# Two neighbouring tokens per partition, regrouping copies within SBUF and a written engine order in a chunked linear-attention and token-mixing kernel

## The chip, the cores and the metric

The kernel runs on one core of one Trainium2 chip. The metric is device time in microseconds of one execution. The kernel before took 166.44 us (median of 3 runs, 164.67 to 166.62).

## The reference

Inputs are `r`, `k`, `v`, `w` of shape (4 batches, 8 heads, 768 tokens, 48) in float32, a bonus `u` of (8, 48), and three small weight matrices. A recurrent linear attention with a decay per channel gives x of (4, 768, 384), and a token-mixing stage gives the output:

```python
for t in range(S):
    cur = np.einsum('bhd,bhe->bhde', u[None] * kt, vt)
    y[:, :, t] = np.einsum('bhd,bhde->bhe', rt, state + cur)
    state = wt[:, :, :, None] * state + np.einsum('bhd,bhe->bhde', kt, vt)
...
W_tok = scale * np.einsum('bsd,btd->bst', x @ w_q, x @ w_k)
mixed = np.einsum('bst,btd->bsd', W_tok, x)
out = np.maximum(mixed, 0.0) @ w_out
```

## The kernel before

The work is cut into 12 blocks of 256 tokens, three to a batch; a block holds two chunks of 128 tokens. For each block `load` (L119) issues eight transfers on the SP queue, two for each of w, k, r and v: 128 tokens on 128 partitions, eight heads of 48 float32 (rows of 192 bytes) each. The pool `ld` has four buffers, so loads can run four blocks ahead.

`prep` (L136) takes the logarithm of w on ACT (`logw`, L142). PE multiplies it with triangular matrices, which gives running sums over the tokens: `cw1` (exclusive) and `cw0` (inclusive, with eight column sums behind it). ACT takes their exponentials (`ecwx` L148, `emcw` L156, and the chunk's decay `pt` L158). DVE forms `Rd` = r times `ecwx` (L162), POOL forms `Kd` = k times `emcw` (L164), ACT casts v to bf16 (`VB`, L167).

`back` (L171) transposes `Rd` and `Kd` on PE (`psT`), DVE copies them out (`RKT`, L179), PE multiplies them to one score matrix `A` per chunk, and DVE masks it into `AmB` (L189, one instruction per chunk). POOL forms k·u (L194) and then ·r (L197) in `uk`, DVE reduces that to `diag` (L199), and POOL makes the bonus rows `Vd` (L201).

`scan` (L205) keeps the state `SB`: for each chunk PE makes `Sn` and the output `Y`, DVE evacuates them (L226, L238) into `X`. Then X is transposed (`xt_ps`, `XT` on ACT, L247) and projected (`qk`, `wk_s`, `wqT`). After a batch's third block `moe` (L260) runs: `Tps`, six `mps` with a Relu on ACT (`mixT`, L272), six `fps` evacuated by DVE and ACT in turn (`osb`, L280 and L282), and the stores on the ACT queue (L283).

PSUM is shared by tags of two buffers each: "big" holds `cw1`, `cw0`, `psT` and both `A`; "s" holds `Sn` and `Y`; "m" holds everything of the projections and of `moe`. A tile takes the buffer of the one before the last, and its first writer waits until that one's readers are done. The main loop (L288) calls `prep(n)` before `back(n - 1)`, so the order of "big" is the sums of block n, then `psT` and `A` of block n - 1. The order on each engine is otherwise chosen by the scheduler of the framework. The framework also gives each transfer of the SP and ACT queues one of eight completion semaphores in turn; a transfer waits until the transfer that had the semaphore before has landed, even when that one stands on the other queue.

Of the kernel before, what the change touches and what calls it, by code (L numbers as in the profile page):

```python
# [25 lines left out]
def kernel(  # L26
# [14 lines left out]
    C = 128  # L41
    NCH = S // C
    NP = H // 2
    NU = S // (2 * C)
# [9 lines left out]
    def mm(o, l, rr, start=True, stop=True, sgc=True, trans=False):  # L54
        nc.tensor.matmul(o, l, rr, start=start, stop=stop,  # L55
                         skip_group_check=sgc, is_transpose=trans)

    nc.scalar.preload_act_table_set("natural_log_exp_and_others")

    consts = ctx.enter_context(tc.tile_pool(name="consts", bufs=1))  # L60
    U128 = consts.tile([C, C], BF16, tag="U128")
    make_upper_triangular(nc, U128, 1.0, diag=True)
    US128 = consts.tile([C, C], BF16, tag="US128")
    make_upper_triangular(nc, US128, 1.0, diag=False)
    ID128 = consts.tile([C, C], BF16, tag="ID128")
    make_identity(nc, ID128)
    ones = U128[:, C - 1:C]

    iota0 = consts.tile([C, 1], mybir.dt.int32, tag="iota0")
    nc.gpsimd.iota(iota0, pattern=[[0, 1]], base=0, channel_multiplier=1)  # L70
    iota1 = consts.tile([C, 1], mybir.dt.int32, tag="iota1")
    nc.gpsimd.iota(iota1, pattern=[[0, 1]], base=1, channel_multiplier=1)
    bias_px = consts.tile([C, 1], F32, tag="bpx")
    bias_mi = consts.tile([C, 1], F32, tag="bmi")
    bias_c = consts.tile([C, 1], F32, tag="bc")
    nc.scalar.activation(bias_px, iota0, ACT.Copy, bias=0.0, scale=MU)
    nc.scalar.activation(bias_mi, iota1, ACT.Copy, bias=0.0, scale=-MU)
    nc.gpsimd.memset(bias_c, MU * C)

    NB = 4
    LW, RdS, KdS, PT = [], [], [], []
    for i in range(NB):
        for lst, nm, e in ((LW, "logw", nc.gpsimd), (RdS, "RdS", nc.vector),
                           (KdS, "KdS", nc.gpsimd)):
            t = consts.tile([C, 2, NP, C], BF16, name=f"{nm}{i}", tag=f"{nm}{i}")
            e.memset(t, 0.0)
            lst.append(t)
        t = consts.tile([C, 2, H], F32, name=f"pt{i}", tag=f"pt{i}")  # L90
        nc.vector.memset(t, 0.0)
        PT.append(t)
# [8 lines left out]
    ld = ctx.enter_context(tc.tile_pool(name="ld", bufs=4))  # L101
# [6 lines left out]
    mout = ctx.enter_context(tc.tile_pool(name="mout", bufs=4))  # L108
# [4 lines left out]
    def stile(shape, dtype, name):  # L113
        return ps.tile(shape, dtype, name=name, tag="s", bufs=2)

    def big(shape, dtype, name):
        return ps.tile(shape, dtype, name=name, tag="big", bufs=2)

    def load(n):  # L119
        b, m = divmod(n, NU)  # L120
        G = {}
        for nm, ap in (("w", w), ("k", k), ("r", r), ("v", v)):
            t = ld.tile([C, 2, H, D], F32, name=nm + "G", tag=nm + "G")
            for c in range(2):
                nc.sync.dma_start(out=t[:, c], in_=ap[  # L125
                    b, :, ds((m * 2 + c) * C, C)].rearrange("h p d -> p h d"))
            G[nm] = t
        return G

    def chd(t):  # L130
        return t

# [3 lines left out]
    def prep(n, G):  # L136
        P = {}
        logw = LW[n % NB]
        Rd = RdS[n % NB]
        Kd = KdS[n % NB]  # L140
        pt = PT[n % NB]
        nc.scalar.activation(pad(logw), chd(G["w"]), ACT.Ln, bias=0.0, scale=LN_SCALE)  # L142
# [62 lines left out]
    def scan(n, P, st):  # L205
# [8 lines left out]
        for cc in range(2):  # L214
# [25 lines left out]
            if c + 1 < NCH:  # L240
                st["S"] = SB2
# [93 lines left out]
```

## Time and profile before

| | |
|---|---|
| median of 3 runs | 166.44 us |
| the profiled execution's own time | 165.66 us |
| its span in the profile | 163.9 us (1.76 us lie around it) |
| busy: PE, DVE, POOL, ACT | 104.8, 99.2, 95.7, 80.9 us |
| transfers of the SP queue | 100242 packets, 18.98 MB |
| stores | 24 of 192 KB, 2.0 us from issue to landing (median) |

In a row of the timeline the first number is the start in us, the second the length (of all the instructions, where the row ends in x2 or more), and a bracket tells how long the engine was idle before and what the profile holds for the releaser. In a row that groups instructions the columns are busy time in us, mean length in ns, idle time before and its releasers.

### The profile page before, as it was taken

Reading aid. Unit: us, or ns where it says so; the run is one execution under the profiler, and the core shown is the slowest. Engines: PE = TensorE matmul, PEld = TensorE weight load, DVE = VectorE, ACT = ScalarE, POOL = GpSimd, SP = SyncE. Lnnn points to the kernel's source line nnn. Section 1 sums busy time; section 2 is a strip of 40 time slices with the busy share of each in tenths; the row PEclk is TensorE's granted clock in tenths of the full one; section 3 lists DMA queues with packets and bytes.
Section 4 is the critical chain, followed back from the end, with each engine's and each line's share of the span. In section 5 each row is a group of like instructions: output and inputs, shape, how many; then the busy total and the mean of one; then the engine's idle time right before and its main releaser. Section 6 shows DMA issues by size and latency. Waiting matters only on the chain.

```text
span 163.9 us, 3082 instructions
## 1 busy us (share of the span) xinstructions
PE 104.8 (64%) x1196; PEld 70.8 (43%) x1196; DVE 99.2 (61%) x124; ACT 80.9 (49%) x152; POOL 95.7 (58%) x72
## 2 busy tenths in 40 slices
PE   0305103752379488994958898886589949857690
PEld 0203003441257365674637366665344527734240
DVE  4020203645668997899889978899582696670030
ACT  3535420430155576775729757793766342303721
POOL 7931009999994999598696952949960940000000
PEclk9999999999999999998799999699975995765967
DMA  5999999999999990289989969999970331000034
GB/s 111 194 187 187 190 187 186 182 210 172 192 183 190 167 175 0 72 221 268 194 165 190 174 173 256 220 197 187 159 140 0 110 125 59 4 0 0 0 127 161
DMA packets 104512, 24.23 MB, mean 148 GB/s; under 512 B 101041, under 2 KB 104498, under 8 KB 104498
## 3 DMA queue, kind: packets, MB, share of 16 engines
q1 hardware_dynamic: 100242, 18.98, 75.0%
q10 hardware_dynamic: 3456, 4.72, 8.2%
q0 software_dynamic: 800, 0.34, 1.7%
q8 instruction: 9, 0.15, 0.4%
q14 instruction: 5, 0.04, 0.1%
HBM read 19.66 MB, written 4.72 MB: 149 GB/s over the span
## 4 chain that ended last, share of the span: by engine, by line
PE 29%; SPq 16%; POOL 15%; DVE 14%; issue 10%; ACT 7%; DMA 6%; ACTq 0%; POOLq 0%
SPq L125 15%; DMA rG<-in_r_dram 6%; DVE AmB L189 6%; PE fps L55 6%; POOL uk L197 5%; PE Y L55 5%; POOL uk L194 4%; PE qk L55 3%; PE psT L55 3%; DVE RKT L179 3%; PE cw L55 3%; POOL KdS L164 3%; POOL Vd L201 3%; PE Tps L55 3%; ACT XT L247 2%
## 5 line engine op out<-in xcount | busy, mean ns | idle before, releaser
L164 POOL TENSOR_TENSOR KdS<-kG,emcw 128x768 bf16<-128x768 f32 x12 | 21.1, 1758 | 18.9 <-ACT emcw L156 11.1
L189 DVE TENSOR_TENSOR AmB<-A,US 128x1024 bf16<-128x1024 f32 x24 | 28.3, 1219 | 4.4 <-PE A L55 4.3
L162 DVE TENSOR_TENSOR RdS<-rG,ecwx 128x768 bf16<-128x768 f32 x12 | 17.2, 1433 | 14.5 <-DMA rG<-in_r_dram 13.4
L197 POOL TENSOR_TENSOR uk<-uk,rG 128x768 f32<-128x768 f32 x12 | 24.3, 2028 | 0.5
L201 POOL TENSOR_TENSOR Vd<-VB,diag 128x768 bf16<-128x768 bf16 x12 | 18.4, 1532 | 10.0 <-DVE diag L199 6.0
L194 POOL TENSOR_TENSOR uk<-kG,ubc 128x768 f32<-128x768 f32 x12 | 21.7, 1810 | 1.7 <-DMA kG<-in_k_dram 1.7
L179 DVE COPY RKT<-psT 128x2048 bf16<-128x2048 bf16 x12 | 14.6, 1218 | 11.1 <-PE psT L55 11.1
L247 ACT COPY XT<-xt_ps 128x768 bf16<-128x768 bf16 x12 | 9.6, 798 | 20.8 <-PE xt_ps L55 20.6
L238 DVE TENSOR_TENSOR X<-Y,Vd 128x384 bf16<-128x384 f32 x24 | 13.2, 552 | 9.2 <-PE Y L55 5.9
L55 PEld LDWEIGHTS <-KdS 128*128 128x128 bf16 x176 | 13.7, 113 | 11.5 <-POOL KdS L164 9.4
L55 PE MATMUL Y<-VB,AmB 128*128 128x48 bf16 x192 | 10.7, 199 | 11.7 <-DVE AmB L189 9.8
L148 ACT ACTIVATE ecwx<-cw,bias_px 128x768 bf16<-128x768 f32 x12 | 10.8, 902 | 14.2 <-PE cw L55 14.2
L55 PEld LDWEIGHTS <-RKT 48*128 48x128 bf16 (+1 forms) x272 | 12.3, 105 | 10.7 <-DVE RKT L179 7.4
L55 PE MATMUL fps<-wout_sb,mixT 128*128 128x384 bf16 x72 | 15.9, 365 | 0.7 <-ACT osb L282 0.3
L55 PE MATMUL cw<-logw,US 128*128 128x384 bf16 x24 | 8.2, 438 | 12.5 <-ACT logw L142 12.5
L55 PEld LDWEIGHTS <-AmB 128*128 128x128 bf16 x192 | 8.4, 107 | 17.6 <-DVE AmB L189 14.8
L55 PE MATMUL psT<-ID,KdS 128*128 128x128 bf16 x96 | 9.4, 242 | 9.1 <-POOL KdS L164 9.1
L199 DVE TENSOR_REDUCE diag<-uk 128x16 f32<-128x768 f32 x12 | 11.4, 946 | 6.3 <-POOL uk L197 6.3
L280 DVE COPY osb<-fps 128x384 f32<-128x384 f32 x12 | 6.7, 554 | 14.0 <-PE fps L55 14.0
L167 ACT CAST VB<-vG 128x768 bf16<-128x768 f32 x12 | 10.0, 830 | 10.3 <-DMA vG<-in_v_dram 10.1
L55 PE MATMUL A<-RKT 48*128 48x128 bf16 x192 | 10.5, 235 | 6.2 <-DVE RKT L179 5.6
L142 ACT ACTIVATE logw<-wG 128x768 bf16<-128x768 f32 x12 | 10.1, 843 | 6.6 <-DMA wG<-in_w_dram 6.5
(54 smaller groups left out, 196.9 us busy)
## 6 DMA issues: line engine op xcount, KB each, us to landing
wG<-in_w_dram SPq DMA_DIRECT2D x24, 192.0 KB, 4.6
kG<-in_k_dram SPq DMA_DIRECT2D x24, 192.0 KB, 4.5
rG<-in_r_dram SPq DMA_DIRECT2D x24, 192.0 KB, 4.5
vG<-in_v_dram SPq DMA_DIRECT2D x24, 192.0 KB, 4.7
out_dram<-osb ACTq DMA_DIRECT2D x24, 192.0 KB, 2.0
wout_sb<-in_moe_w_out_dram POOLq DMA_DIRECT2D x1, 288.0 KB, 6.1
wq_f<-in_moe_w_q_dram SPq DMA_DIRECT2D x1, 96.0 KB, 4.1
wk_sb<-in_moe_w_k_dram POOLq DMA_DIRECT2D x1, 48.0 KB, 4.3
```

The lines of the kernel that those rows point to most:

```text
L55: nc.tensor.matmul(o, l, rr, start=start, stop=stop, skip_group_check=sgc, is_transpose=trans)
L125: nc.sync.dma_start(out=t[:, c], in_=ap[b, :, ds((m * 2 + c) * C, C)].rearrange("h p d -> p h d"))
L162: nc.vector.tensor_tensor(pad(Rd), chd(G["r"]), ecwx.rearrange("p c (h d) -> p c h d", d=D), ALU.mult)
L164: nc.gpsimd.tensor_tensor(pad(Kd), chd(G["k"]), emcw.rearrange("p c (h d) -> p c h d", d=D), ALU.mult)
L179: nc.vector.tensor_copy(RKT, psT)
L189: nc.vector.tensor_tensor(AmB[:, c].rearrange("p q h t -> p h q t"), A, _rep(_rep(US128, 1, NP), 1, 2), ALU.mult)
L194: nc.gpsimd.tensor_tensor(uk, G["k"], _rep(ubc.rearrange("p (h d) -> p h d", d=D), 1, 2), ALU.mult)
L197: nc.gpsimd.tensor_tensor(uk, uk, G["r"], ALU.mult)
L199: nc.vector.tensor_reduce(diag, uk, axis=AX.X, op=ALU.add)
L201: nc.gpsimd.tensor_tensor(Vd, VB, _rep(diag, 3, D), ALU.mult)
L238: nc.vector.tensor_tensor(X[:, c], Y8, P["Vd"][:, cc].rearrange("p h d -> p (h d)"), ALU.add)
L247: nc.scalar.copy(XT[:, :, ds(m * 2 * C, 2 * C)], tp)
```

## The change

- **Layout.** A block's 256 tokens lie with tokens 2p and 2p+1 on partition p. One transfer per input and block then has rows of 384 bytes: `load` issues four per block instead of eight. Halves of the partitions now hold the two chunks. `ld` has three buffers instead of four.
- **Sums.** Over this layout PE needs two matmuls for each of three sums (`cwa`, two halves, and `cwb`), six per block instead of four; the exponentials are four instructions of 384 columns instead of two of 768.
- **Transposes** need nothing more: `trR` writes each transposed 128 columns to the two chunks' places.
- **Regrouping.** The second operand role of k, v and the bonus rows needs one chunk on 128 partitions. `Kd`, `VB` and `Vd` of a block stand side by side in one tile (`KdS`, 1280 columns), and `swap` copies it into `Kn` with four transfers of 64 partitions by 2560 bytes on the SP queue.
- **Stores** are two per pair of chunks, each from 64 partitions.
- **Set-up.** Only the gaps of the padded tiles are zeroed (256 columns of `KdS` on POOL, where `KdS` and `logw` had 1024 each); masks and biases follow the new layout. The load of `w_q` moves from the SP queue to POOL's.
- **Order.** Every step has a time in a table, and the instructions are written in the order of these times; the scheduler no longer moves them. A block is 8.3 units long; the sums of block n + 1 (at 9.2) come after the score matrices of block n (7.2 and 7.8).

```diff
-    ld = ctx.enter_context(tc.tile_pool(name="ld", bufs=4))
+    ld = ctx.enter_context(tc.tile_pool(name="ld", bufs=3))
...
+    def load(n, nm, ap):
+        b, m = divmod(n, NU)
+        src = ap[b, :, ds(m * C2, C2)]
+        t = ld.tile([C, H, D2], F32, name=nm + "G", tag=nm + "G")
+        nc.sync.dma_start(out=t, in_=src.rearrange("h (p j) d -> p h (j d)", j=2))
+        T[nm, n] = t
...
+    def sums(n):
+        lw = LW[n % NB]
+        lw4 = pad(lw)
+        cwa = big([C, 2, 512], F32, "cwa")
+        cwb = big([C, 2, 512], F32, "cwb")
+        for o, m0, m1 in ((cwa[:, 0], BS, BS), (cwa[:, 1], BI, BS), (cwb[:, 0], BI, BI)):
+            od = o[:, 0:DM].rearrange("p (h d) -> p h d", d=D)
+            mm(od, m0, lw4[:, 0], stop=False)
+            mm(od, m1, lw4[:, 1], start=False)
...
+    def exps(n):
+        cwa, cwb = T["cwa", n], T["cwb", n]
+        ex = hw.tile([C, 2, DM], BF16, name="ex", tag="ex")
+        em = hw.tile([C, 2, DM], BF16, name="em", tag="em")
+        nc.scalar.activation(em[:, 0], cwa[:, 1, 0:DM], ACT.Exp, bias=bias[2], scale=-1.0)
+        nc.scalar.activation(em[:, 1], cwb[:, 0, 0:DM], ACT.Exp, bias=bias[3], scale=-1.0)
+        nc.scalar.activation(ex[:, 0], cwa[:, 0, 0:DM], ACT.Exp, bias=bias[0], scale=1.0)
+        nc.scalar.activation(ex[:, 1], cwa[:, 1, 0:DM], ACT.Exp, bias=bias[1], scale=1.0)
...
+    def swap(n):
+        Kn = bt.tile([C, 2, KV], BF16, name="Kn", tag="Kn")
+        for q in range(2):
+            for j in range(2):
+                nc.sync.dma_start(out=Kn[ds(j * HC, HC), q],
+                                  in_=KdS[n % NB][ds(q * HC, HC), j])
...
+    def vd(n):
+        nc.gpsimd.tensor_tensor(vpart(KdS[n % NB], 1), vpart(KdS[n % NB], 0),
+                                _rep(T["diag", n], 3, D), ALU.mult)
...
+        steps = [
+            (-3.2, uk1, ()), (-0.7, log, ()), (0.2, uk2, ()), (0.9, sums, ()),
+            (2.0, exps, ()), (2.6, red, ()), (3.0, kdec, ()),
+            (3.9, decay, ()), (4.0, rdec, ()), (2.4, vcast, ()), (4.9, trR, (1,)),
+            (5.2, vd, ()), (5.4, trR, (0,)), (6.0, evT, ()), (6.8, swap, ()),
+            (7.2, amat, (0,)), (7.7, mask, (0,)), (7.8, amat, (1,)), (8.9, mask, (1,)),
+        ]
```

In this table `uk1` and `uk2` are the two products for the bonus, `kdec` and `rdec` make `Kd` and `Rd`, `trR` the transposes (1 for k, 0 for r), `evT` the copy to `RKT`, `amat` and `mask` the score matrix and its mask, `decay` makes `pt`. A second table puts `state` and `ymat` with their evacuations `stev` and `yev` 12.5 and more after a block's start, and the stage behind a batch (`tmat`, `mix`, `fin` with their evacuations) after its last block.

The rows below are instruction orders; a name's number tells buffers apart. **DVE, from one `AmB` of an early block to the next block's.** Before, `RdS_102` belongs to block 2 and stands ahead of the copy `RKT` of block 1:

```order
L189 TENSOR_TENSOR AmB<-A,US_64 128x2x4x128 x2
L199 TENSOR_REDUCE diag<-uk 128x16
L226 TENSOR_TENSOR SB_300<-Sn,pt_90 128x384
L162 TENSOR_TENSOR RdS_102<-rG,ecwx 128x16x48
L238 TENSOR_TENSOR X<-Y_284,Vd 128x384
L238 TENSOR_TENSOR X<-Y_302,Vd 128x384
L179 COPY RKT<-psT 128x2048
```

The same place now; `RdS_79` belongs to block 2, and so do the `RKT` and the `AmB` behind it:

```order
L226 TENSOR_TENSOR AmB<-A,MASK 128x2x4x128
L243 TENSOR_REDUCE diag<-uk 128x8x2
L175 TENSOR_TENSOR RdS_79<-rG,ex 128x16x48
L268 TENSOR_TENSOR SB_515<-Sn,pt_77 128x384
L296 TENSOR_TENSOR X<-Y,Kn 128x384
L211 COPY RKT<-psT 128x2048
L296 TENSOR_TENSOR X<-Y,Kn 128x384
L226 TENSOR_TENSOR AmB<-A,MASK 128x2x4x128
L268 TENSOR_TENSOR SB_574<-Sn,pt_77 128x384
```

What moved: the decayed r (and on PE the sums) of a block stood one block ahead of its transposes and now stand in the same block.

**ACT, in block 1**, where the weight `wq_sb` waits for its load, and `pt_77` is what frees the PSUM buffer of block 1's first score matrix:

```order
L188 CAST KdS_76<-vG 128x2x384
L415 ACTIVATE wq_sb<-wq_f 128x192
L169 ACTIVATE pt_77<-cwb,bias_c 48x4x2 x2
L137 ACTIVATE logw_78<-wG 128x16x48
L310 COPY XT<-xt_ps 128x3x256
```

Before, `pt_98` of block 1 stood ahead of `wq_sb`:

```order
L158 ACTIVATE pt_98<-cw_203,bias_c 48x8 x2
L167 CAST VB<-vG 128x768
L297 ACTIVATE wq_sb<-wq_f 128x192
L142 ACTIVATE logw_100<-wG 128x16x48
L167 CAST VB<-vG 128x768
```

What moved: `wq_sb` now stands between the cast of v and the two `pt` of block 1.

**ACT, in the block after the Relus of a batch** (`em` and `ex` are the exponentials of the next block):

```order
L310 COPY XT<-xt_ps 128x3x256
L367 COPY osb<-fps 128x384
L373 DMA out_dram<-osb 64x2x384 x2
L159 ACTIVATE em<-cwa,bias_67 128x384
L160 ACTIVATE em<-cwb,bias_68 128x384
L161 ACTIVATE ex<-cwa,bias_65 128x384
L162 ACTIVATE ex<-cwa,bias_66 128x384
L328 CAST wk_s<-qk 128x128
L329 CAST wqT<-qk 64x256
L188 CAST KdS_76<-vG 128x2x384
L367 COPY osb<-fps 128x384
```

What moved: one evacuation and two stores stand ahead of the exponentials, and the next evacuation behind the cast of v.

451 lines of the change are left out of this document (263 added, 188 removed).

## The prediction

> **What bounds the kernel now.** I read the queues first, then the masks as a clock of the blocks, then the idle time at the start. The page, and the SP queue's own waits and timeline:
>
> ```profile
> DMA  5999999999999990289989969999970331000034
> q1 hardware_dynamic: 100242, 18.98, 75.0%
> SPq L125 <- DMA out_dram<-osb: 15.5, 2, 11.3
> 57.14 1.55 SPq L125 DMA_DIRECT2D rG<-in_r_dram  x2
> 70.03 1.12 SPq L125 DMA_DIRECT2D vG<-in_v_dram  x2
> ```
>
> The transfer engines look like the bound: nines for 30 of 40 slices. But in slices 15 and 16 they are empty, because a load waited 11.3 us for a store's semaphore (from 58.7 to 70.0). What that full queue costs is read from the blocks. The DVE timeline, first and last masks, one quick pair, and the last X:
>
> ```profile
> 29.16 2.36 DVE L189 TENSOR_TENSOR AmB<-A,US 128x1024 bf16<-128x1024 f32 x2 [0.31 <-PE A L55]
> 47.10 2.36 DVE L189 TENSOR_TENSOR AmB<-A,US 128x1024 bf16<-128x1024 f32 x2 [1.35 <-PE A L55]
> 83.76 2.36 DVE L189 TENSOR_TENSOR AmB<-A,US 128x1024 bf16<-128x1024 f32 x2 [0.79 <-PE A L55]
> 91.61 2.36 DVE L189 TENSOR_TENSOR AmB<-A,US 128x1024 bf16<-128x1024 f32 x2
> 143.16 2.35 DVE L189 TENSOR_TENSOR AmB<-A,US 128x1024 bf16<-128x1024 f32 x2 [0.22 <-PE A L55]
> 146.43 0.56 DVE L238 TENSOR_TENSOR X<-Y,Vd 128x384 bf16<-128x384 f32 x1 [0.45 <-PE Y L55]
> ```
>
> Masks of the first block end at 31.5, of the last at 145.5: 114.0 us for 11 intervals, 10.4 each. One interval took 17.9, a quick one 7.85, so the middle is held near 8 by DVE and stretched by stalls. Ahead lie 31.5 us, behind 18.4. Why 31.5? The POOL timeline:
>
> ```profile
> 8.74 0.95 POOL L88 MEMSET KdS<- 128x1024 bf16 x1
> 15.90 0.68 POOL L293 PARTITION_BROADCAST ubc<-u  x1 [6.21 <-ACT ecwx L148]
> 24.40 3.23 POOL L164 TENSOR_TENSOR KdS<-kG,emcw 128x768 bf16<-128x768 f32 x2 [7.82 <-DMA kG<-in_k_dram]
> ```
>
> POOL idles 6.2 us before the broadcast and 7.8 us behind it. The inputs of the first `KdS` were there long before 24.4: k of block 0 was issued by 3.4. [...]
>
> **The change part by part. Start.** [...] POOL's set-up shrinks: of eight fills of 0.95, four remain with a quarter of the columns, and some nine small mask instructions come, so it ends near 5.5 instead of 9.7 (estimate). Then 6.2 + 0.7 + 7.8 gives 20.2. The bonus products now stand ahead of `Kd`; their prices and those of the block's chain:
>
> ```profile
> L194 POOL TENSOR_TENSOR uk<-kG,ubc 128x768 f32<-128x768 f32 x12 | 21.7, 1810 | 1.7 <-DMA kG<-in_k_dram 1.7
> L201 POOL TENSOR_TENSOR Vd<-VB,diag 128x768 bf16<-128x768 bf16 x12 | 18.4, 1532 | 10.0 <-DVE diag L199 6.0 <-ACT wqT L257 2.0 <-ACT VB L167 1.9
> 80.48 1.65 POOL L164 TENSOR_TENSOR KdS<-kG,emcw 128x768 bf16<-128x768 f32 x1 [1.63 <-ACT emcw L156]
> L189 DVE TENSOR_TENSOR AmB<-A,US 128x1024 bf16<-128x1024 f32 x24 | 28.3, 1219 | 4.4 <-PE A L55 4.3
> L179 DVE COPY RKT<-psT 128x2048 bf16<-128x2048 bf16 x12 | 14.6, 1218 | 11.1 <-PE psT L55 11.1
> L226 DVE TENSOR_TENSOR SB<-Sn,pt 128x384 bf16<-128x384 f32 x20 | 11.0, 549 | 0.2
> L199 DVE TENSOR_REDUCE diag<-uk 128x16 f32<-128x768 f32 x12 | 11.4, 946 | 6.3 <-POOL uk L197 6.3
> L272 ACT ACTIVATE mixT<-mps 128x384 bf16<-128x384 f32 x24 | 10.8, 489 | 2.1 <-PE mps L55 1.7
> 85.43 0.49 PE L55 MATMUL cw<-logw,US 128*128 128x384 bf16 x2
> 71.80 0.61 PE L55 MATMUL psT<-ID,KdS 128*128 128x128 bf16 x8
> 74.71 0.42 PE A L55 x8
> ```
>
> Two products 3.6, `Kd` 1.65, transposes 0.7 with the hops, `RKT` 1.2, `A` 0.5, two masks 2.35: the first masks end at **30.2**.
>
> **A plain interval.** This is the heart. Before, a block's sums and both decayed operands were made one block ahead. Now the order of the PSUM tag is sums, transposes, scores of the same block, and the second sum `cwb` of block n + 1 takes the buffer of the second `A` of block n. So one chain runs through every block, counted from the end of a second mask: two matmuls for `cwb` 0.6 with hops; one exponential of 384 columns 0.5 (like a Relu of that size): 1.1; `Kd` 1.7: 2.8. DVE's decayed r is ready at 2.0, but meets `Kd`:
>
> ```profile
> 70.89 1.82 POOL L194 TENSOR_TENSOR uk<-kG,ubc 128x768 f32<-128x768 f32 x1
> 71.00 2.52 DVE L162 TENSOR_TENSOR RdS<-rG,ecwx 128x768 bf16<-128x768 f32 x1
> 72.79 2.40 POOL L197 TENSOR_TENSOR uk<-uk,rG 128x768 f32<-128x768 f32 x1
> ```
>
> DVE's product began behind POOL's, ended 0.8 after it, and POOL's next was 0.6 longer: they exclude each other. So it ends at 3.65. `SB` and X of the block before follow in DVE's order (0.9): 4.55, hiding the transposes of r; `RKT` 1.2: 5.75; `A` 0.5: 6.25; mask 1.2; `SB` 0.4; mask 1.2: **9.05**; 8.6 where a block has no second `SB`. DVE's own work would fit in about 7.5, the sum of the same rows without the waits. There are two of the one, three of the other: 43.9. The bound above is POOL's next product slipping in first each time, 1.8 more; below, no exclusion, 0.8 less. I keep the middle row's order.
>
> **Intervals with a batch's stage.** Six of the eleven carry it. Prices:
>
> ```profile
> L167 ACT CAST VB<-vG 128x768 bf16<-128x768 f32 x12 | 10.0, 830 | 10.3 <-DMA vG<-in_v_dram 10.1
> L266 ACT CAST Tsb<-Tps 64x384 bf16<-64x384 f32 x4 | 1.9, 473 | 4.0 <-PE Tps L55 4.0
> L282 ACT COPY osb<-fps 128x384 f32<-128x384 f32 x12 | 5.8, 479 | 10.1 <-PE fps L55 8.1 <-DVE osb L280 2.0
> 68.02 0.86 ACTq L283 DMA_DIRECT2D out_dram<-osb  x2
> 82.60 0.80 PE qk L55 x9
> 70.00 0.50 PE fps L55 x3
> ```
>
> In the first (three of them) PE reaches the first `mps` only when ACT has cast v (to 3.2) and `Tsb` (3.7); `Sn`, `Y`, the transposes and two more `mps` follow in PE's order, so `RKT` starts at 5.8 instead of 4.55; three `mps`, `Sn` and `Y` then stand ahead of `A`: first mask at 7.75 instead of 6.25; one `osb` on DVE between the masks, 0.5: **11.05**. In the second, one `osb` and two store issues (0.5 + 0.9) stand ahead of the exponentials on ACT (+0.6); PE must pass four `fps` before `Sn`, the last waiting for the `osb` behind the cast of v (4.3), so the transposes end at 6.65; DVE waits for an `osb` before the decayed r, which then meets the next POOL product (to 5.2) and ends at 6.05; `RKT` at 6.95: **11.5**. Together 3 x 22.55 = 67.65. Bounds: each at 9.05 if the slack swallows all, each 2 longer if the waits add.
>
> **Weights.** `wq_sb` stands ahead of `pt` of block 1 on ACT and waits for a load that POOL issues only behind `Kd` of block 1 (at 2.8).
>
> ```profile
> wk_sb<-in_moe_w_k_dram POOLq DMA_DIRECT2D x1, 48.0 KB, 4.3
> L158 ACT ACTIVATE pt<-cw,bias_c 48x8 f32<-48x8 f32 x24 | 6.2, 260 | 1.3 <-DVE osb L280 1.1
> ```
>
> Landing at 7.1, `wq_sb` 0.4, two `pt` 0.5, `A` 0.5: first mask at 8.5 instead of 6.25, **+2.3** once (0 if the load lands within 2 us).
>
> **Loads and copies.** 384-byte rows move between 187 GB/s (nothing gained per byte: 8.4 us per block) and twice that (the packet as unit: 4.2). The nearest row is of stores in 1536-byte rows, the window from 155 to 164:
>
> ```profile
> GB/s 0 0 0 0 0 0 0 0 0 0 0 0 55 362 369 348 403 212 0 116 348 362 48 48 355 382 89 246 348 396 348 369 41 0 0 0 0 0 0 0
> out_dram<-osb ACTq DMA_DIRECT2D x24, 192.0 KB, 2.0
> wG<-in_w_dram SPq DMA_DIRECT2D x24, 192.0 KB, 4.6
> ```
>
> I take 4.2 to 6: hidden under 9 to 11 us of block. The four copies (0.66 MB, 1.8 us at the stores' rate) wait for `Vd`, which ends 2.4 us before an interval begins; PE wants the first two at 2.3, so 4.7 us later. A store lands in 2.0, a load in a full ring in 4.6: I take 2.6 for two copies, hidden; without that cover it costs one for one. On SP they stand ahead of the loads three blocks on, which have 12 us of slack; a load or copy can still wait for a store's semaphore, and this slack covers it. [...]
>
> **Tail.** 18.4 as before; the last two X now follow the last mask at once (+0.1), and the last store leaves as a pair behind the last evacuation: 0.4 for another issue and some 0.6 of transfer. **19.5**.
>
> **Sum.** 30.2 + 43.9 + 67.65 + 2.3 + 19.5 = 163.55 of span; the profiled execution lay 1.76 over its span (165.66), so 165.3; said as **165**. That execution lies 0.8 under the median of 166.44, and 2% of that, about what a measurement of this kernel can tell, is 3.3 us.
>
> **Rivals.** (a) The written order hides the batch's stage: every interval stays near 9, and the weights land in time. 165.3 - 6 intervals' excess of 13.35 - 2.3 = 150. For it: DVE has 1.5 us free per block and ACT and PE more. Against: PE, ACT and DVE each take their instructions in order, and the named waits stand ahead of the transposes. (b) POOL's gaps are waits for inputs after all: `Kd` of block 0 would start near 10.6 (k landed by 7, two products 3.6) instead of 23.8: 152. Against: the inputs were there. (c) Slower: the copies land late. [...] It decides from 4.7 us after `Vd`. For it: copies and loads share the ring. Against: the ring is mostly empty by then. (d) 384-byte rows gain nothing per byte: 8.4 + 3.5 for the copies + 1 for stores = 12.9 per block, 180. Against: the stores' 348 to 403 GB/s.
>
> **How the numbers follow.** The forecast has 0.45: 0.30 within 2%, 0.10 faster and 0.05 slower, since its terms are uncertain by some 6 us (159 to 171, its own range). (a) 0.27, (b) 0.06, (c) 0.16, (d) 0.06. Faster: 0.10 + 0.27 + 0.06 = 0.43; within 2%: 0.30; slower: 0.05 + 0.16 + 0.06 = 0.27. The range goes from (a) to (c): 149 to 174, which leaves (d) and edges out.
>
> **What would show it.** Right: POOL's two gaps again, first masks ending near 30; `KdS` waiting for the exponential of `cwb` in every block; plain masks 9 apart and those with a batch's stage 11 to 12; the transfer digits no longer all nines; `Sn` not waiting for copies. Wrong: masks evenly 8 to 9 apart (a); first masks before 20 (b); PE waiting for `Kn` in plain blocks (c); loads landing later than 8 us behind their issue (d).

## The result and the profile after

The changed kernel took 175.03 us (median of 4 runs, 174.32 to 178.33) beside 165.56 for the kernel before on the same chip: ratio 1.056 (95% interval 1.044 to 1.069), so slower by some 9.5 us. The forecast was 165.0 with a range to 174. Later comparisons are ratios to the kernel before on the chip of that run, with runs of a disturbed clock left out; medians contain all runs.

The profiled execution took 175.48 us with a span of 173.7. First the lines that answer to those of before: the transfer engines and SP's queue on the page, and two DMA issue groups (KB each, median us from issue to landing).

```profile
DMA  5999300499794989947999898399965053740055
q1 hardware_dynamic: 53762, 26.75, 58.3%
...
Kn<-KdS SPq DMA_DIRECT2D x48, 160.0 KB, 2.8
...
out_dram<-osb ACTq DMA_DIRECT2D x24, 192.0 KB, 3.0
```

The transfers are no longer a wall of nines, although the queue now moves 26.75 MB with the copies instead of 18.98. POOL's timeline at the start:

```profile
4.11 1.07 POOL L406 MEMSET KdS<- 128x256 bf16 x4
12.21 0.68 POOL L411 PARTITION_BROADCAST ubc<-u  x1 [7.03 <-issue]
22.17 1.79 POOL L232 TENSOR_TENSOR uk<-kG,ubc 128x768 f32<-128x768 f32 x1 [9.29 <-issue]
...
25.80 1.64 POOL L185 TENSOR_TENSOR KdS<-kG,em 128x768 bf16<-128x768 f32 x1
```

Both gaps are there again, now with "issue" for a releaser, that is with nothing that the profile could name. They are larger: 7.03 and 9.29, together 16.3 where I had used 14.0. DVE's timeline, of the first block and then of a plain one:

```profile
25.88 0.95 DVE L243 TENSOR_REDUCE diag<-uk 128x16 f32<-128x768 f32 x1 [22.90 <-POOL uk L238]
26.75 1.50 DVE L175 TENSOR_TENSOR RdS<-rG,ex 128x768 bf16<-128x768 f32 x1
29.42 1.23 DVE L211 COPY RKT<-psT 128x2048 bf16<-128x2048 bf16 x1 [1.17 <-PE psT L58]
31.35 2.36 DVE L226 TENSOR_TENSOR AmB<-A,MASK 128x1024 bf16<-128x1024 f32 x2 [0.71 <-PE A L58]
...
54.41 1.22 DVE L226 TENSOR_TENSOR AmB<-A,MASK 128x1024 bf16<-128x1024 f32 x1
...
57.94 1.55 DVE L175 TENSOR_TENSOR RdS<-rG,ex 128x768 bf16<-128x768 f32 x1 [1.45 <-ACT ex L162]
...
62.06 2.36 DVE L226 TENSOR_TENSOR AmB<-A,MASK 128x1024 bf16<-128x1024 f32 x2
```

The first masks end at 31.35 + 2.36 = 33.71 (forecast 30.2). A block's second mask ends at 55.63 and the next one's at 64.42: 8.79 for a plain interval (forecast 8.6). The ends of all second masks, read in this way, cut the span into the windows of the next table. Its columns are the window, its length, the busy time and number of instructions of PE, PEld (PE's weight loads), DVE, ACT and POOL, TensorE's granted clock (PEclk, 1.00 is full speed), the share of the DMA engines and GB/s.

```profile
0.00:33.71 33.71, 6.27 (x50) 4.18 (x51) 7.91 (x28) 6.22 (x10) 15.64 (x32) 1.00 0.56 148
33.71:46.06 12.35, 8.33 (x83) 6.00 (x82) 7.95 (x10) 5.31 (x11) 9.18 (x7) 1.00 0.99 231
46.06:55.63 9.57, 7.50 (x95) 5.27 (x95) 7.76 (x10) 5.86 (x12) 7.33 (x4) 1.00 0.79 210
55.63:64.42 8.79, 5.87 (x90) 4.22 (x90) 7.31 (x9) 4.75 (x10) 7.33 (x4) 0.95 0.97 252
64.42:76.37 11.95, 10.22 (x109) 6.36 (x108) 8.62 (x10) 9.04 (x19) 7.32 (x4) 0.90 0.90 231
76.37:88.68 12.31, 8.28 (x109) 5.57 (x107) 8.99 (x12) 6.83 (x15) 7.32 (x4) 1.00 0.82 234
97.45:109.02 11.57, 9.31 (x108) 5.77 (x108) 8.62 (x10) 8.90 (x19) 7.33 (x4) 1.00 0.91 238
109.02:122.14 13.12, 9.56 (x109) 6.97 (x107) 9.09 (x12) 6.82 (x15) 7.33 (x4) 0.87 0.85 248
154.63:173.70 19.07, 9.93 (x66) 4.79 (x62) 3.25 (x6) 5.90 (x14) 0.00 (x0) 0.88 0.24 63
```

In these windows no engine is full: in the plain one DVE and POOL work 7.3 of 8.79 us, in the one with `mps` (64.42 to 76.37) PE and ACT 10.2 and 9.0 of 11.95. I take it that the chain of waits sets the time; the experiments on the order test this. I call the two kinds with a batch's stage M (with `mps`, here 11.95 and 11.57) and F (with most `fps` and the stores, 12.31 and 13.12). The eleven intervals sum to 120.9 where the forecast had 113.85.

| | forecast | measured |
|---|---|---|
| first masks end | 30.2 | 33.71 |
| first interval (weights) | 11.35 | 12.35 |
| plain intervals | 9.05, 8.6 x3 | 9.57, 8.79, 8.77, 8.78 |
| M, three times | 11.05 | 11.95, 11.57, 11.56 |
| F, three times | 11.5 | 12.31, 13.12, 12.15 |
| tail | 19.5 | 19.07 |
| span | 163.55 | 173.70 |

So +3.5 at the head, +1.0 in the first interval, +1.1 in the plain ones, +1.9 in M, +3.1 in F, and -0.4 in the tail: +10.1.

The same reading of the kernel before tells where the change lost. Its masks gave 31.5 us for the head, 17.9 for the first interval and 18.4 for the tail, which leaves 96.1 for the other ten intervals; now these are 33.7, 12.4, 19.1 and 108.6. So the changed kernel gains 5.6 us in the first interval and loses 12.5 in the ten others, 2.2 at the head and 0.7 in the tail.

### The profile page after: what moved, and what is told of

Same layout as the page of the kernel before. It is cut to its first block, busy times and chain, and to the rows that moved or that the text cites. A ratio compares the mean times of both kernels' runs of the same rounds, so it can differ in the third digit from the quotient of the medians.

```text
span 173.7 us, 3187 instructions
## 1 busy us (share of the span) xinstructions
PE 104.7 (60%) x1220; PEld 69.2 (40%) x1220; DVE 101.8 (59%) x138; ACT 84.2 (48%) x174; POOL 93.9 (54%) x77
## 3 DMA queue, kind: packets, MB, share of 16 engines
q1 hardware_dynamic: 53762, 26.75, 58.3%
## 4 chain that ended last, share of the span: by engine, by line
PE 24%; DVE 23%; ACT 17%; issue 12%; POOL 7%; SPq 7%; DMA 6%; ACTq 2%; DVEq 0%; POOLq 0%
DVE AmB L226 10%; SPq L133 6%; DVE RKT L211 5%; PE fps L58 4%; PE cwb L58 4%; DVE SB L268 4%; DMA rG<-in_r_dram 3%; PE mps L58 3%; ACT em L160 3%; PE A L58 3%; ACT ex L162 3%; PE psT L58 3%; DMA wq_f<-in_moe_w_q_dram 3%; POOL uk L232 2%; ACTq L373 2%
## 5 line engine op out<-in xcount | busy, mean ns | idle before, releaser
L185 POOL TENSOR_TENSOR KdS<-kG,em 128x768 bf16<-128x768 f32 x12 | 19.6, 1637 | 36.6 <-ACT em L160 36.6
L226 DVE TENSOR_TENSOR AmB<-A,MASK 128x1024 bf16<-128x1024 f32 x24 | 28.9, 1220 | 3.1 <-PE A L58 2.9
L175 DVE TENSOR_TENSOR RdS<-rG,ex 128x768 bf16<-128x768 f32 x12 | 19.3, 1609 | 12.6 <-ACT ex L162 12.6
L159 ACT ACTIVATE em<-cwa,bias 128x384 bf16<-128x384 f32 x12 | 7.0, 581 | 34.7 <-PE cwa L58 30.4
L248 POOL TENSOR_TENSOR KdS<-KdS,diag 128x768 bf16<-128x768 bf16 x12 | 19.1, 1591 | 0.4 <-ACT KdS L188 0.4
L58 PE MATMUL cwa<-logw,BS 128*128 128x384 bf16 x36 | 11.8, 387 | 10.2 <-POOL KdS L406 5.2
L369 DVE COPY osb<-fps 128x384 f32<-128x384 f32 x12 | 6.7, 555 | 19.1 <-PE fps L58 19.1
L296 DVE TENSOR_TENSOR X<-Y,Kn 128x384 bf16<-128x384 f32 x24 | 13.1, 548 | 0.9 <-PE Y L58 0.8
L352 ACT ACTIVATE mixT<-mps 128x384 bf16<-128x384 f32 x24 | 11.4, 490 | 4.5 <-PE mps L58 4.4
L58 PEld LDWEIGHTS <-mixT 128*128 128x128 bf16 x72 | 7.0, 103 | 16.2 <-issue 14.1
L137 ACT ACTIVATE logw<-wG 128x768 bf16<-128x768 f32 x12 | 10.1, 843 | 5.3 <-DMA rG<-in_r_dram 2.8
L268 DVE TENSOR_TENSOR SB<-Sn,pt 128x384 bf16<-128x384 f32 x20 | 11.0, 549 | 1.9 <-PE Sn L58 1.9
```

The source lines that it names most:

```text
L58: nc.tensor.matmul(o, l, rr, start=start, stop=stop, skip_group_check=True, is_transpose=trans)
L175: nc.vector.tensor_tensor(pad(RdS[n % NB]), jhd(T["r", n]), hd(T["ex", n]), ALU.mult)
L185: nc.gpsimd.tensor_tensor(pad(Kd), jhd(T["k", n]), hd(T["em", n]), ALU.mult)
L226: nc.vector.tensor_tensor(T["AmB", n][:, c].rearrange("p q h t -> p h q t"), T["A", n, c], _rep(_rep(MASK, 1, NP), 1, 2), ALU.mult)
L248: nc.gpsimd.tensor_tensor(vpart(KdS[n % NB], 1), vpart(KdS[n % NB], 0), _rep(T["diag", n], 3, D), ALU.mult)
L268: nc.vector.tensor_tensor(SB2.rearrange("p (h d) -> p h d", d=D), T["Sn", n, cc].rearrange("p (h d) -> p h d", d=D), _rep(PT[n % NB][:, cc ...
```

## The experiments

Every edit starts from the changed kernel, except where the text names another.

### The two gaps of POOL

```diff
-        nc.sync.dma_start(out=u1, in_=u.rearrange("h d -> (h d)"))
-        nc.gpsimd.partition_broadcast(ubc, u1)
+        nc.sync.dma_start(out=ubc, in_=_rep(u.rearrange("h d -> (h d)"), 0, C))
```

In the changed kernel, whose gaps are 7.03 and 9.29 us, to see whether they go with the broadcast:

> The changed kernel, but u reaches all 128 partitions by one transfer with a repeated source row instead of POOL's broadcast. [...] Rival (the gaps are waits for inputs): the decayed k of block 0 still starts after 20 us, and the time stays at 172 to 178.

Measured: 163.03 us (10 runs), ratio to before 0.994 (0.981 to 1.007). POOL's timeline of that kernel:

```profile
7.72 1.80 POOL L232 TENSOR_TENSOR uk<-kG,ubc 128x768 f32<-128x768 f32 x1 [2.87 <-DMA kG<-in_k_dram]
...
11.37 1.63 POOL L185 TENSOR_TENSOR KdS<-kG,em 128x768 bf16<-128x768 f32 x1
```

With no broadcast in the program, both gaps are gone and only a wait of 2.87 us for k's real landing is left: `KdS` starts at 11.37 instead of 25.80, 14.4 earlier. The time falls by 12.0 us. Rival (b), that the gaps were waits for inputs, falls. What POOL does in them no run shows; shown is that both vanish with the broadcast. The same edit in the kernel before, whose first decayed keys (`KdS`) start at 24.40:

> The kernel before, with the bonus row u sent to all partitions by one transfer in place of GpSimd's broadcast. [...] Rival (before's start is set by its loads of small rows, which land late, so that GpSimd's gaps are covered by them): the keys start at most 5 us sooner and the time falls by less than 4, 161 to 166.

Measured: 157.98 us, ratio 0.959 (0.946 to 0.971). POOL's first product there, then the logarithm (ACT) and the sums (PE) of block 1, and the first masks (DVE):

```profile
9.35 2.21 POOL L164 TENSOR_TENSOR KdS<-kG,emcw 128x768 bf16<-128x768 f32 x1
...
14.29 0.84 ACT L142 ACTIVATE logw<-wG 128x768 bf16<-128x768 f32 x1 [2.42 <-DMA wG<-in_w_dram]
...
15.18 0.80 PE L55 MATMUL cw<-logw,US 128*128 128x384 bf16 x2 [7.75 <-ACT logw L142]
...
21.85 2.34 DVE L189 TENSOR_TENSOR AmB<-A,US 128x1024 bf16<-128x1024 f32 x2
```

`KdS` starts at 9.35 instead of 24.40, but the first masks end at 24.19 instead of 31.52, only 7.3 us sooner: in PE's order the sums of block 1 stand ahead of the transposes, and they wait until 15.18 for a load of w. The time falls by 8.4. So the gaps were a cost of both kernels, some 8 us before and 12 after: the kernel before hid part of them under its loads, the changed one pays 3.6 us more for them. In the kernel before the scheduler also chose other orders for the engines with this edit, and the 8.4 holds both.

### Row length and regrouping copies

Two transfers of 192-byte rows in place of one of 384:

```diff
-        nc.sync.dma_start(out=t, in_=src.rearrange("h (p j) d -> p h (j d)", j=2))
+        for j in range(2):
+            nc.sync.dma_start(out=t[:, :, ds(j * D, D)],
+                              in_=src.rearrange("h (p j) d -> j p h d", j=2)[j])
```

> The changed kernel, but each load is cut into two transfers with rows of 192 bytes (one for the even tokens, one for the odd), as small as those of the kernel before; tiles, copies and order are the same. Theory (transfers are hidden behind blocks of 9 to 12 us): loads take 8.3 us per block again, with 2 to 3 us for the copies and 1 to 2 for the stores, so they come close to the block's length: 0 to 10 us more, 174 to 185. Rival (the 384-byte rows carry the change, transfers bound it): 20 us and more on top.

Measured: 181.93 us, ratio 1.114 (1.097 to 1.130). The rates of the changed kernel, then of this one:

```profile
GB/s 135 285 296 287 84 0 0 120 276 223 175 323 104 266 233 257 241 122 188 318 276 309 203 295 214 95 263 360 275 166 147 4 151 92 205 131 0 0 133 140
```

```profile
GB/s 113 204 217 212 218 85 68 227 186 230 209 178 225 214 234 186 206 261 182 209 229 209 193 212 222 205 259 247 248 161 247 25 146 88 174 150 0 0 129 133
```

While only loads run, in the second to the fourth of the 40 slices, 384-byte rows give 285 to 296 GB/s and 192-byte rows 204 to 217 in the same kernel. Beside 175.03 and 177.29 (the changed kernel again, below) the longer rows are worth 5 to 7 us here. Rival (d) falls. Without the regrouping copies (the state and output products read `KdS` where it stands, so the regrouping is left out):

```diff
-        Kn = bt.tile([C, 2, KV], BF16, name="Kn", tag="Kn")
-        for q in range(2):
-            ...
+        Kn = KdS[n % NB]
```

> The changed kernel without the regrouping copies: the state and output products read the tile of POOL and ACT in place. It leaves the regrouping out, so the products mix tokens of the two chunks; shapes and instruction counts of the engines are the same. Theory (copies are hidden behind the block): the time stays within 1.5%, 172 to 177. Rival (copies land late, or hold up loads and stores): 5 us or more faster.

Measured: 176.72 us, ratio 1.080 (1.061 to 1.099). No gain: in the changed kernel the copies are hidden (PE waited for one once in its profile, 0.22 us), and rival (c) does not explain its time.

### Stores, weights

The stores' issue moved from ACT to SP, in `store`:

```diff
-            nc.scalar.dma_start(
+            nc.sync.dma_start(
```

> The changed kernel with the stores issued by SyncE in place of ScalarE, at the same places of the order. Theory (ScalarE is in the chain during a batch's final products and its store issues of 1.3 us a pair delay the exponentials behind them): the three intervals with stores lose about 1.3 each, 170.5 to 172 us. Rival A (ScalarE's store issues are hidden behind other waits of the chain): no difference, 174 to 176. Rival B (on SyncE the stores wait for the output buffers and hold up the regrouping copies and loads that stand behind them): 177 or more.

Measured: 175.4 us, ratio 1.064 (1.050 to 1.077): no difference in the whole time, as rival A has it. The windows tell more: an F interval, a later one, and the tail. The last row is ACT's, the exponential of `cwb` in the first of these F intervals.

```profile
74.58:85.62 11.04, 8.29 (x109) 5.58 (x107) 8.99 (x12) 6.72 (x15) 7.31 (x4) 1.00 1.01 296
106.86:117.91 11.05, 8.29 (x109) 5.57 (x107) 9.00 (x12) 6.76 (x15) 7.32 (x4) 1.00 0.98 283
...
149.90:172.00 22.10, 14.11 (x73) 6.96 (x73) 3.35 (x6) 5.90 (x14) 0.00 (x0) 0.58 0.24 62
...
75.37 0.57 ACT L160 ACTIVATE em<-cwb,bias 128x384 bf16<-128x384 f32 x1
```

The F intervals fell from 12.31 and 13.12 to 11.04 and 11.05, as the theory said. The tail, 22.10 instead of 19.07, took most of it back: the granted clock there was 0.58 instead of 0.88, and the same kind of products kept PE busy 14.11 us instead of 9.93. Leaving out the stores of three batches:

```diff
-            for i in range(3):
+            for i in range(3 if b == B - 1 else 0):
```

> The changed kernel without the stores of the first three batches (their outputs are left out; the products and their evictions stay). Theory: the intervals that held the stores fall from a mean of 12.5 to 11, and with three of them the time to 169.5 to 171.5. Rival (the length of these intervals comes from the final products and their evictions, which wait for each other over two PSUM buffers, and the stores stand beside it): 174 to 176.

Measured: 175.26 us (171.34 to 176.47): too scattered to tell anything by the whole time. The F interval from 106.99 to 118.04 in its windows is again 11.05 at a clock of 1.00, as much as with the stores on SP. Beside the F intervals of the changed kernel at that clock, 12.31 and 12.15, the stores' part is 1.1 to 1.3; the third, 13.12, lies in a window at 0.87, and how much of the rest is the clock is not separated:

```profile
106.99:118.04 11.05, 8.29 (x109) 5.58 (x107) 9.00 (x12) 6.76 (x15) 7.31 (x4) 1.00 0.76 197
```

ACT's timeline of the changed kernel shows the place:

```profile
75.97 0.48 ACT L367 COPY osb<-fps 128x384 f32<-128x384 f32 x1 [0.73 <-PE fps L58]
76.48 1.36 ACTq L373 DMA_DIRECT2D out_dram<-osb  x2
77.95 0.58 ACT L159 ACTIVATE em<-cwa,bias 128x384 bf16<-128x384 f32 x1 [1.50 <-PE qk L58]
78.43 0.57 ACT L160 ACTIVATE em<-cwb,bias 128x384 bf16<-128x384 f32 x1
```

The first exponential starts when the issue of two stores (1.36) is through; the profile's releaser (`qk` on PE) is not the cause. The exponential of `cwb` ends at 79.00, 2.63 behind the second mask (76.37); with the stores on SP it ends at 75.94, 1.36 behind it (74.58), as in a plain interval (1.33). Next, the scaling of the query weights, taken out of `wload` and put behind the first block's `XT`:

```diff
+    at(17.4, lambda: nc.scalar.activation(wq_sb, wq_f, ACT.Copy, bias=0.0, scale=scale))
```

> The changed kernel with ScalarE's scaling of the query weights moved behind the first block's copy of the transposed result, so that it no longer waits 4.5 us for the weights' landing ahead of the second block's exponentials; the transfers of the weights stay where they are. Theory (this wait is the 2 to 3 us by which the first interval exceeds a plain one): 171.8 to 173.3. Rival (the first interval is long because GpSimd issues the three weight transfers ahead of the second block's work, and that stays): 174.5 to 176.

Measured: 174.94 us, ratio 1.066 (1.055 to 1.078); again nothing in the whole time. Its windows:

```profile
32.01:42.30 10.29, 8.32 (x83) 5.92 (x82) 7.96 (x10) 5.20 (x11) 8.34 (x7) 1.00 1.02 237
...
151.23:172.90 21.67, 12.79 (x72) 6.24 (x69) 3.35 (x6) 5.90 (x14) 0.00 (x0) 0.66 0.21 55
```

The first interval fell by 2.06, from 12.35 to 10.29, and the tail rose by 2.6, to 21.67, at a clock of 0.66. Both single mends hold in their stage and vanish in the sum. To see whether such tails come with the clock, the changed kernel ran again, unaltered, on the chip of a later experiment:

> The changed kernel itself, unaltered, on the same chip as the run beside it. If the tail of 21 to 22 us of some experiments against 19.1 of the changed kernel, and plain or stage intervals of one kernel that differ by 0.3 to 2 us, go with the granted clock and not with the edits, then this kernel shows them too where its clock is under 0.8: a tail of 20.5 to 22 at such a clock, near 19 otherwise, and 174 to 177 us in all.

Measured: 177.29 us, ratio 1.068 (1.054 to 1.082). Its second M interval and its last window:

```profile
97.49:109.81 12.32, 10.87 (x110) 6.65 (x109) 8.53 (x10) 9.14 (x19) 7.31 (x4) 0.85 0.86 223
...
155.72:176.00 20.28, 11.25 (x66) 5.22 (x62) 3.25 (x6) 5.90 (x14) 0.00 (x0) 0.75 0.23 59
```

The same program has a tail of 19.07 at a clock of 0.88 and of 20.28 at 0.75 (I had expected 20.5 or more), and the same M interval of 11.57 at 1.00 and 12.32 at 0.85. Of the other kernels whose tail is written in the same order, the two with a clock over 0.8 had tails of 18.9 and 19.5 us, the five between 0.58 and 0.76 had 19.7 to 22.1. So one us of a whole time, by the other kernels up to three, can go with the clock of the tail; what sets that clock no run shows. I therefore compare intervals where the clock is 1.00. The three edits together:

> The changed kernel with three edits together: the bonus row by transfer, the stores issued from SyncE, the scaling of the query weights behind the first block's copy. In the single profiles they took 14.4 us from the first block, 1.1 to 2.1 from each interval with stores and 2.1 from the first interval; the tail was 19 to 22 us, with the granted clock. Theory (the three are separate terms and add up): first masks end at 19.3, intervals sum to 115.4, so 155.5 to 158.5 us, as much as the kernel before with the bonus row by transfer (158.0). Rival (what one saves is waited for elsewhere once the transfers of the loads are no longer ahead): 160 to 163.

Measured: 161.13 us (158.8 to 162.52): only 1.9 less than with the bonus row alone, in the rival's range. The profile again divides: intervals at a clock of 1.00 are as expected, and two others and the tail are long at a low clock.

```profile
59.16:70.19 11.03, 8.28 (x109) 5.57 (x107) 8.98 (x12) 6.71 (x15) 7.31 (x4) 1.00 1.03 301
78.97:92.59 13.62, 11.36 (x102) 6.66 (x102) 8.68 (x11) 8.48 (x18) 7.31 (x4) 0.69 0.96 253
92.59:106.38 13.79, 11.31 (x114) 6.89 (x114) 8.41 (x12) 7.36 (x15) 7.32 (x4) 0.81 0.72 196
```

The M interval from 78.97 takes 13.62 at 0.69, against 11.56 at 1.00 in the changed kernel. Whether the mends themselves bring the low clock on was not settled.

### The order: one block ahead

The transposes, scores and masks of a block moved 6.5 units later, behind the next block's sums (which moved 0.65 earlier), and the second table by 2.3 (`L` from 4.0 to 6.3):

```diff
-            (3.9, decay, ()), (4.0, rdec, ()), (2.4, vcast, ()), (4.9, trR, (1,)),
+            (3.9, decay, ()), (5.3, rdec, ()), (2.4, vcast, ()), (11.5, trR, (1,)),
...
-            (7.2, amat, (0,)), (7.7, mask, (0,)), (7.8, amat, (1,)), (8.9, mask, (1,)),
+            (13.7, amat, (0,)), (14.2, mask, (0,)), (14.3, amat, (1,)), (15.4, mask, (1,)),
```

> The changed kernel with only its order edited: transposes, scores, masks and all that follows come one block later in the table, and the sums of the next block a little earlier, so that a block's sums, exponentials and both decayed operands are made one block ahead of its transposes, as in the kernel before. Layout, copies and loads are the same. Theory (the PSUM buffers of the tag for sums, transposes and scores tie the sums, the decayed k and r, transposes, copy and masks of a block into one chain of 9 us and more per block): that chain loses the decayed k and r, plain intervals between masks fall from 8.8 to 9.6 us to about 8 to 8.4, the whole by 8 to 14 us, to 161 to 167. Rival (the copies within SBUF, or transfers, cost the time): no change beyond 2%, 172 to 178.

Measured: 177.43 us, ratio 1.083 (1.062 to 1.104): a miss, no gain. Two plain windows and one with a stage:

```profile
50.27:58.18 7.91, 5.85 (x96) 4.31 (x95) 7.28 (x11) 5.27 (x11) 7.33 (x5) 1.00 0.99 259
58.18:66.43 8.25, 6.82 (x92) 4.55 (x91) 6.92 (x9) 6.39 (x14) 7.68 (x5) 1.00 1.04 279
66.43:81.24 14.81, 11.64 (x115) 6.80 (x115) 8.73 (x13) 7.69 (x19) 7.79 (x5) 0.88 0.55 133
```

Where the clock was 1.00 the plain intervals did fall, from 8.79 to 7.9 and 8.25, so the chain through one block is real; two later ones, where PEclk on the page goes down to 6 and 8 tenths, took 9.7. But the first masks ended later (41.5), and in this profile, of a run of 181 us, an interval with a stage grew to 14.8, another to 16.4, at clocks of 0.88 and 0.79. In PE's order the `fps` now stood between the transposes and the scores, and waited there up to 0.8 us at a time for ACT and DVE; I read that as the reason, though these waits and the low clock were not told apart.

### The order: the batch's stage

So the stage was moved instead, with the three mends kept: `mps` and `fps` in pairs at three places of a period where PE would wait anyway: behind the sums, behind the transposes, behind the scores. The stores' places and the engine of one evacuation in six move with them.

```diff
-            tb = t0 + L + 15.0
-            bsteps = [(0.0, tmat, ()), (0.5, tev, ())]
+            tb = t0 + 2 * P
+            bsteps = [(2.4, tmat, ()), (2.9, tev, ())]
             for i in range(6):
-                bsteps += [(1.2 + 0.7 * i, mix, (i,)), (1.6 + 0.7 * i, mixev, (i,))]
...
+                g, e = i // 2, i % 2 * 0.01
+                bsteps += [((4.5, 6.1, 7.85)[g] + e, mix, (i,)),
+                           ((4.6, 6.2, 8.02)[g] + e, mixev, (i,)),
+                           (P + (3.0, 6.1, 7.85)[g] + e, fin, (i,)),
+                           (P + (4.1, 6.3, 8.02)[g] + e, finev, (i, i not in (0, 2)))]
...
+                bsteps += [(P + (6.9, 8.3, 10.0)[i], store, (i,))]
```

> As the kernel with the three edits, and the batch's stage written in pairs at three places of each period where TensorE and ScalarE stand idle (behind the cumulative sums, behind the copy of the transposes, behind the attention products), instead of in one row of products 0.7 to 0.8 apart. Theory (the stage's 2.8 and 2.3 us over a plain interval are waits of TensorE, in its written order, for ScalarE's evictions over two PSUM buffers, not work that has no room): the six intervals fall to 9.5 to 10.1, 146.5 to 149.5 us. Rival (the stage's products and evictions have no room beside the chain wherever they stand): 155 to 158.

Measured: 151.97 us, ratio 0.903 (0.890 to 0.917), the fastest kernel of the case and 9 us under the three mends alone, of which 2.9 lie in the tail (18.41 at a clock of 0.96 instead of 21.34 at 0.68); it is 2.5 above the expected range. The kernel before took 162.52 to 168.21 in six runs on that chip, so by its fastest run the ratio would be 0.94. The windows: one M, one F, and an M in which PE waited 1.15 us for a copy and the clock was 0.86; the third M was like it, 12.28:

```profile
48.39:58.79 10.40, 8.13 (x104) 5.08 (x103) 7.97 (x11) 8.80 (x19) 7.32 (x4) 0.98 0.93 245
58.79:68.84 10.05, 8.61 (x113) 6.00 (x113) 8.60 (x13) 7.00 (x15) 7.33 (x4) 1.00 0.84 221
...
77.63:89.74 12.11, 9.28 (x102) 5.93 (x102) 8.12 (x10) 8.73 (x19) 7.32 (x4) 0.86 1.01 278
```

Both orders together, one block ahead and the stage spread at places that fit it:

```diff
-            bsteps = [(2.4, tmat, ()), (2.9, tev, ())]
+            bsteps = [(4.7, tmat, ()), (5.0, tev, ())]
...
-                bsteps += [((4.5, 6.1, 7.85)[g] + e, mix, (i,)),
+                bsteps += [((6.1, 7.5, 8.65)[g] + e, mix, (i,)),
...
-                           (P + (3.0, 6.1, 7.85)[g] + e, fin, (i,)),
+                           (P + (4.6, 6.1, 7.5)[g] + e, fin, (i,)),
```

> As the kernel with the spread stage, and the sums, exponentials and decays written one block ahead of the transposes, attention products and masks, as in the first experiment, whose plain intervals were 7.9 to 8.2 and whose intervals with a batch's stage were 9.4 to 16.4. Theory (with the stage out of the chain's way, all intervals come near the busy time of VectorE and GpSimd, 7.3): 7.9 to 9 for all eleven, first masks at 22 to 25, 138 to 145 us. Rival (written one block ahead, the stage's buffers and evictions still stop TensorE in the middle of the chain): intervals with the stage over 11, 150 us or more.

Measured: 158.97 us, ratio 0.950 (0.939 to 0.962): the rival. In its profile F and the later plain intervals are 7.5 to 8.4, but M is 12.8 to 14.0, at clocks of 0.87 and 0.88: what was spared in F came back in M. Then the spread by itself, on the changed kernel, with the broadcast, the scaling and the stores' engine as they were, and the last store issue of a batch behind the next block's exponentials:

```diff
-                bsteps += [(7.4 + 1.6 * i, store, (i,))]
+                bsteps += [(P + (4.75, 6.9, 12.25)[i], store, (i,))]
```

> The changed kernel with one thing altered: the batch's stage written in pairs at three places of each period, and each store issue behind its pair and behind the period's exponentials. The broadcast of the bonus row, the scaling of the query weights and the stores' engine stay. Theory (the place of the stage and of the stores in the written order is by itself what makes the changed kernel slower than the one before): first masks near 33 as in the changed kernel, the six intervals at 10 to 10.5 instead of 11.6 to 13.1, 164 to 167 us, no slower than before. Rival (the stage costs what it costs wherever it stands, and the kernel with the spread stage was fast by its other edits and by its clock): 171 to 175.

Measured: 170.6 us, ratio 1.018 (1.001 to 1.036): between the two, and still no faster than the kernel before. Two windows, then PE's timeline in the second, then the SP queue's waits (total, times, longest):

```profile
72.22:82.27 10.05, 7.97 (x111) 5.71 (x111) 8.60 (x13) 5.64 (x13) 7.32 (x4) 1.00 0.71 172
...
114.32:126.72 12.40, 7.44 (x95) 5.64 (x93) 7.57 (x9) 5.91 (x12) 7.31 (x4) 0.83 1.11 318
```

```profile
119.76 0.50 PE L58 MATMUL Sn<-Kn 128*128 128x96 bf16 x4 [3.37 <-DMA Kn<-KdS]
```

```profile
SPq L133 <- DMA out_dram<-osb: 13.4, 2, 6.7
```

The six intervals with a stage sum to 62.3 instead of 72.7, 10.4 less, as expected. But two plain intervals grew, by 2.0 and 3.6: in the second PE waits 3.37 us for a regrouping copy. On SP's queue the copies stand behind loads, and twice a load waited for the semaphore of a store, up to 6.7 us, where the changed kernel has four such waits and the longest is 5.2; I had moved the last stores later myself. The tail, 21.29 instead of 19.07, took another 2.2. Without the copies (left out as above):

> The kernel with the spread stage alone, without the regrouping copies: the state and output products read the decayed keys and values where they stand, with rows in the wrong order (the regrouping is left out, the work of the products is the same). Theory (the spread took 10.4 us from the six intervals, and TensorE's three waits of 7.3 us for the copies in the two plain intervals gave half of it back, because with shorter periods the copies stand behind late loads in the queue): the plain intervals return to 8.8, the six stay at 10 to 10.5, 163.5 to 166.5 us. Rival (what was given back lies in something else in these intervals, such as the store issues or the granted clock): 169 or more.

Measured: 167.58 us, ratio 1.012 (1.001 to 1.023); 1 us above the theory's range, below the rival's.

```profile
84.47:93.66 9.19, 6.30 (x94) 4.42 (x93) 7.29 (x9) 5.90 (x12) 7.32 (x4) 0.94 0.94 258
...
114.34:123.54 9.20, 6.06 (x94) 4.26 (x93) 7.30 (x9) 6.06 (x13) 7.32 (x4) 1.00 0.36 88
```

The two intervals are back at 9.2, from 10.75 and 12.40, so late copies had given back 4.8 of the 10.4 us. Rival (c) of the prediction, copies that land late, showed here, with shorter blocks and later loads ahead of the copies: between 82 and 128 us PE waited for them three times, 7.3 us in all, in the kernel with the copies, where in the changed kernel it did so once, 0.22 us.

## Why the prediction was wrong, point by point

The mechanism was the one forecast, a chain of waits through each block with POOL's gaps ahead of it. What failed is the size of its terms, 10.1 us in sum: above all the head (+3.5) and F (+3.1).

- **POOL's gaps stay: right**, and sized too small. The step "6.2 + 0.7 + 7.8" took the gaps of before as fixed durations, which was my assumption: the runs show only that they go with the broadcast. They were 7.03 and 9.29, and the set-up ended 0.3 earlier, +2.0 in all. Part of that is chance: of the nine other profiles with the broadcast at the head of the changed kernel, one has a gap of 6.9 ahead and three have 7.4, 8.0 and 8.6 behind it, and in all nine the first product starts at 19.7 to 22.2, in the middle 20.8, where the forecast had 20.2 and this profile 22.2.
- **The first block's chain: one link was left out.** I went from `Kd` straight to the transposes. But in DVE's written order the decayed r stands behind `diag`, which waits for POOL's second product. So it starts 0.95 behind `KdS` and takes 1.50 (26.75 to 28.25), and then come 1.17 of waiting for PE's last transposes: +1.3. Smaller hops make the other 0.2.
- **The plain interval: right** within 0.2 for the three short ones (8.6 against 8.77 to 8.79), and right step by step: counted from a second mask, the exponential of `cwb` ended at 1.33 (forecast 1.1), the decayed r at 3.86 (3.65), `RKT` at 5.93 (5.75), and the first mask began at 6.43 (6.25). The 0.2 arises at the exponential: it began 0.75 behind the mask instead of 0.6, and took 0.58 where I had put 0.49. With the order one block ahead these intervals fell to 7.9 and 8.25 at full clock, which shows the chain.
- **The weights: right** in kind. +2.3 forecast, 2.06 by experiment. The first interval still was 1.0 too long: its exponential of `cwb` ended 0.5 later than in a plain one, POOL issued the first weight load at 3.5 instead of 2.8, and the scaling began at 8.0 instead of 7.1.
- **M: half a us too short** (11.05 against 11.56 at full clock); no run tells which of its links.
- **F: the term that was mis-sized most among the intervals.** "One `osb` and two store issues (0.5 + 0.9) stand ahead of the exponentials on ACT (+0.6)": a pair of issues took 1.26 to 1.37 (one 1.62) instead of 0.86, from 64 partitions each, and the exponential of `cwb` came 1.0 to 1.3 late instead of 0.6. With the stores on SP it came 0.03 late, and F was 11.04, near the 10.9 that the forecast has without this term. I took the old price for a changed form. The F of 13.12 holds some 0.8 more, in a window at a clock of 0.87.
- **Loads and copies: right** for this kernel: rows of 384 bytes ran at 285 to 296 GB/s, the copies landed in 2.8 (I took 2.6) and were hidden.
- **Tail: right** within 0.4, but I gave it no uncertainty, and in runs of the same order it goes from 18.9 to 22.1, longer where the clock is lower.
- **A reading:** the page of before has nines in 23 of 40 slices, not in 30. No term of the sum hung on it.
- **The range** ended at 174 because rival (c) lies there, and not by any term of the case that came. No run shows copies in the changed kernel as late as 174 takes them for: they landed in 2.8 us (median), and leaving them out gained nothing. The forecast's own range of 6 us to either side treated the small links as errors of both signs. Hops and waits that were left out all lengthen; with the gaps of this execution and the clock they came to +3.5 at the head and +7.1 in the intervals, and only the tail came out shorter, by 0.4.

So the forecast case was the one that came, with its terms 10 us short in sum. In rival (a) I asked whether the written order hides the stage. The order as written doesn't; another order takes 10.4 us from the six intervals, about half of what they are over plain ones.

What the change is worth, where both kernels are rid of the broadcast: 157.98 (ratio 0.959) for the kernel before, 163.03 (0.994) for the changed one, 151.97 (0.903) for the changed one with the stage spread, the stores on SP and the scaling moved. The 384-byte rows gain, as the 192-byte rows in the same kernel show. Whether the layout as a whole gains is not shown: the kernel before was never written in an order of its own, and the spread alone, with the broadcast kept, still took 170.6 us. By their intervals the stage's place costs some 10 us, the shorter rows would cost 5 to 7.

## What to carry to other kernels

When an order is written out by hand, price every instruction that stands ahead of the chain on each engine, DMA issues too, and look for the longest chain through one block; a stage that runs only now and then did better here in pairs where its engines idle than in a row. A price is bound to its form: a pair of stores of 192 KB cost ACT 0.82 to 0.86 us to issue from 128 partitions and mostly 1.26 to 1.37 from 64. Compare stages, not only whole times: a mend of 2.06 us was plain in its interval and lost in a tail 2.6 us longer, at a clock of 0.66 instead of 0.88.

## What the runs showed of the hardware

- A single GpSimd broadcast of 0.68 us went with idle time of 6.21 us ahead of it and 7.82 behind it in the kernel before, and of 7.03 and 9.29 in the changed one; three other profiles of the changed start have 7.4, 8.0 and 8.6 behind it. Without the broadcast both are gone: only a wait of 2.87 us for the load of k is left in the changed kernel, and the first `KdS` starts 14.4 us earlier there and 15.05 earlier in the kernel before.
- Two stores of 64 partitions took ACT mostly 1.26 to 1.37 us to issue where two of 128 took 0.82 to 0.86, and landed in 3.0 us instead of 2.0 (medians).
- Loads alone ran at 285 to 296 GB/s with rows of 384 bytes and at 204 to 217 with rows of 192.
- The granted clock differed between two executions of one program, by window: the changed kernel's second M interval took 11.57 us at 1.00 in one and 12.32 at 0.85 in another, its tail 19.07 at 0.88 and 20.28 at 0.75.
